# Three engines set to the source's order, with attention dealt out by slots and a third weight group in the sums' place

## The chip, the cores and the metric

One core of a Trainium2 chip runs one launch of the kernel. Its engines work in parallel, each on its own queue of instructions, and wait for one another by semaphores: TensorE (PE) multiplies matrices, VectorE (DVE) and ScalarE (ACT) do elementwise work, GpSimd (POOL) does little here, SyncE (SP) issues nearly all DMAs. The metric is device time in microseconds (us), the median of several executions.

## The reference

A transformer block in which attention and a feed-forward part stand side by side, in float32, for 2048 tokens of 576 features:

```python
x = A_x                                   # [1, 2048, 576]
xn = _layernorm(x, axis=-1)
return x + _A_ref(xn, A_wqkv, A_wo) + _B_ref(xn, B_w1, B_b1, B_w2, B_b2)

def _A_ref(x, wqkv, wo):                  # 32 heads of 18, 8 keys each, every second token back
    W, dil = 8, 2
    ...
    idx = pos[:, None] - off[None, :]
    ...
    logits = jnp.einsum("bhsd,bhswd->bhsw", q, kg) * scale
    logits = jnp.where(mask[None, None, :, :], logits, -1e9)
    attn = _softmax(logits, axis=-1)
    o = jnp.einsum("bhsw,bhswd->bhsd", attn, vg)
    return (lambda x, *d: x.transpose(*d))(o, 0, 2, 1, 3).reshape(B, S, D) @ wo

def _B_ref(x, w1, b1, w2, b2):            # 576 -> 4608 -> 576
    h = jnp.einsum("bsd,df->bsf", x, w1) + b1
    r = jnp.where(h > zero, h, zero)
    h = r * r
    return jnp.einsum("bsf,fd->bsd", h, w2) + b2
```

## The kernel before

**Numbers.** TensorE multiplies in a rounded 32-bit format. To keep float32's accuracy each operand is split in two: ScalarE writes the rounded upper half (`split`, lines 105 to 110), VectorE subtracts it from the original for the lower half (all through `tt`, line 103), and a product is three matmuls. So every weight and every activation that TensorE reads needs one ScalarE and one VectorE instruction first.

**Blocks and stages.** The tokens are four blocks of 512. In order: an opening (layer-norm of block 0 and its first Q, K, V weights); `q0`, the Q, K, V rows of blocks 0 and 1 in four groups of eight heads, 14 matmuls a row; `phase_a(0)`; `phase_b0`; `phase_a(1)`; `phase_b1`; `tail`.

**`phase_a(s)`** is 18 pairs (`ffn_pair`) over the 36 tiles of 128 hidden features. A pair computes two tiles for blocks 2s and 2s+1 at once by a scheme with seven products in place of eight (B11, T1, T2, T3, B21, B22, T4; 50 matmuls with the leftover 64 features), which needs sums of weights (`combine_w1`, VectorE) and sums of activations (`sums`, `last_sum`). Between the products `work(0)` to `work(3)` put seven matmuls each of the second layer of the pair before it, for block 2s. For block 2s+1 the hidden features `h` go out to DRAM and are read back (`load_h`) in `phase_b0` or `phase_b1`, which run that block's second layer, 36 tiles of 14 matmuls. `phase_b0` also computes Q, K, V of blocks 2 and 3.

**Attention** (`attention`, line 258) is done on VectorE for 16 pieces (block b, head group g). Q, K and V go to DRAM scratch and come back as `q` (two buffers) and `kv` (three) with the keys that precede a block. For each of four token columns VectorE multiplies queries with eight shifted keys (`pr<-q,kv`) and sums over 18 features (line 272); then a softmax with ScalarE's exponential (line 279); then four times weights by values (`pr<-lg,kv`) and a sum over the eight (line 288). The result goes to scratch. `regroup` (line 460) reads it back in 16 small DMAs a half, VectorE transposes it, and 65 matmuls apply `wo`.

**What sets the order.** Only TensorE's instructions (and those of the opening and the tail) run in the order of the source. VectorE, ScalarE and SyncE are ordered when the program is built, by a scheduler that fills each engine by priority and readiness; attention stands under `lazily`, at a priority below all else, so its pieces fall wherever that scheduler's model finds VectorE free. Once built, each engine's order is fixed.

**Weights.** `w1` tiles are loaded one pair ahead, split in two instructions (`split_w1`); `w2` tiles are loaded three ahead into `w2r` and split into `w2s` two ahead.

Of the kernel before, what the change touches and what calls it, by code (L numbers as in the profile page):

```python
# [8 lines left out]
F32 = mybir.dt.float32  # L9
# [7 lines left out]
P = 128  # L17
# [24 lines left out]
LATE = 1 << 20  # L42
# [4 lines left out]
def block_kernel(ctx: ExitStack, tc: tile.TileContext, x, xt, wqkv, wo, w1, b1, w2, b2, out):  # L47
# [6 lines left out]

    xv = x.rearrange("(b p j) d -> b p j d", p=P, j=NJ)
# [3 lines left out]
    first = sb.tile([P, 2, TB], F32, name="mb")  # L59
    ident, odd = first[:, 0, :P], first[:, 1].bitcast(F32R)  # L60
# [23 lines left out]

    late = [LATE]

    @contextmanager
    def lazily():
        kept = tc.cur_priority
        tc.cur_priority = late[0]  # L90
        yield
        late[0] = tc.cur_priority
        tc.cur_priority = kept
# [28 lines left out]
    def take_left(to, v, t):  # L122
        nc.scalar.activation(to[:64], v[:64], AF.Copy)
        nc.scalar.activation(t[64:], v[64:], AF.Copy)
        tt(to[64:], v[64:], t[64:].bitcast(F32), ALU.subtract)

# [18 lines left out]

    def statistics(b):
        rows = sb.tile([P, NJ, D], F32, name="kv", bufs=3)
        nc.sync.dma_start(rows, xv[b])
        mr = sb.tile([P, 2, NJ], F32, name="mr")
        for j in range(NJ):  # L150
            for k in range(2):
                bn_stats(b, rows, j, k)
# [3 lines left out]
        nc.sync.dma_start(mrscr[b].rearrange("n p -> p n"), mr.rearrange("p k j -> p (k j)"))  # L156

    def load_xt(b):
        xm[b] = sb.tile([P, NC - 1, TB], F32, name="w1r", bufs=2)
        nc.sync.dma_start(xm[b], xt[b, :, :NC - 1])  # L160
        xf[b] = four()[:, 0] if b % 2 else sb.tile([P, TB], F32, name="xf")
        nc.sync.dma_start(xf[b], xt[b, :, NC - 1])
        mb[b] = sb.tile([P, 2, TB], F32, name="mb")
        nc.sync.dma_start(mb[b].rearrange("c k t -> c (k t)"), flat(mrscr[b], 0, [0, P], 2 * NJ * P))

    def normalize(b):
        open_x(b)
        for a in (0, 2):
# [3 lines left out]
            split(X[b][:, 0, a:a + 2], X[b][:, 1, a:a + 2], v)  # L172
        for k, op in enumerate((ALU.subtract, ALU.mult)):
            tt(xf[b], xf[b], mb[b][:, k], op)
        take_left(x4[b], xf[b], four(F32R)[:, 0])

    def sums(s):
# [3 lines left out]
        v = xm[b1]  # L181
        for i in (1, 2, 3):
            SS[i] = mt.tile([P, 2, 2, TB], F32R, name=f"S{i}")
        f = four()
        tt(f, v[:, :2], v[:, 2:], ALU.add)
        split(SS[1][:, 0], SS[1][:, 1], f)
        e = four()
        tt(e, f, hi(0), ALU.subtract)
        tt(e, e, lo(0), ALU.subtract)
        split(SS[2][:, 0], SS[2][:, 1], e)  # L190
        f = four()
        tt(f, hi(0), v[:, :2], ALU.subtract)
        tt(f, f, lo(0), ALU.add)
        split(SS[3][:, 0], SS[3][:, 1], f)
        tt(v[:, :2], hi(2), e, ALU.subtract)
        tt(v[:, :2], v[:, :2], lo(2), ALU.add)
        x4["d"] = mt.tile([P, TB], F32R, name="x4d")
        tt(xf[b1], xf[b0], xf[b1], ALU.subtract)
        take_left(x4["d"], xf[b1], four(F32R)[:, 0])

    def last_sum(s):
        b = 2 * s + 1
        split(X[b][:, 0, :2], X[b][:, 1, :2], xm[b][:, :2])
# [3 lines left out]
    def load_wq(g):  # L207
        raws[g] = []
        for k in range(3):
            n = 2 if k < 2 else 1  # L210
            r = sb.tile([P, 2, QW], F32, name="r4", bufs=4)[:, :n]
            nc.sync.dma_start(r, wqkv[g, :, 2 * k:2 * k + n])
            raws[g].append(r)

    def split_wq(g, name, ks=range(3)):
        for k in ks:
            n = 2 if k < 2 else 1
            t = mt.tile([P, 2, 2, TB], F32R, name=name, bufs=3)[:, :n, :, :QW]
            wq.setdefault(g, []).append(t)
            split(t[:, :, 0], t[:, :, 1], raws[g][k])  # L220
# [3 lines left out]
    def row_products(b, g, j):  # L224
        js = slice(j * P, (j + 1) * P)
        mm = []
        for c in range(NC):
            w = wq[g][c // 2][:, c % 2]
# [29 lines left out]

    def attention(b, g):
        k, v = (sb.tile([P, NE, CG], F32, name="kv", bufs=3) for _ in range(2))  # L260
        q = sb.tile([P, NJ, CG], F32, name="q", bufs=2)
        nc.sync.dma_start(q.rearrange("p j c -> p (j c)"), flat(scr["q"][g], (PAD + b * TB) * CG, [NJ * CG, P], NJ * CG))
        for t, n in ((k, "k"), (v, "v")):
            nc.sync.dma_start(t.rearrange("p e c -> p (e c)"),
                              flat(scr[n][g], (PAD + b * TB - HALO) * CG, [NJ * CG, P], NE * CG))
# [3 lines left out]
        for j in range(NJ):  # L269
            pr = sb.tile([P, W, CG], F32, name="pr")  # L270
            tt(pr, q[:, j:j + 1].to_broadcast([P, W, CG]), shifted(k, j, [1, CG]), ALU.mult)
            nc.vector.tensor_reduce(out=lg[:, j * HG:(j + 1) * HG].rearrange("p a w -> p w a"),  # L272
                                    in_=pr.rearrange("p w (a d) -> p w a d", d=DH), axis=AX.X, op=ALU.add)
        if b == 0:
# [4 lines left out]
        nc.scalar.activation(lg, lg, AF.Exp, scale=SCALE)  # L279
        nc.vector.tensor_reduce(out=sm, in_=lg, axis=AX.X, op=ALU.add)  # L280
        nc.vector.reciprocal(sm, sm)
        tt(lg, lg, sm[:, :, None].to_broadcast([P, NA, W]), ALU.mult)
        for j in range(NJ):
# [4 lines left out]
            nc.vector.tensor_reduce(out=q[:, j], in_=pr.rearrange("p w c -> p c w"), axis=AX.X, op=ALU.add)  # L288
        nc.sync.dma_start(oscr[b, g].rearrange("(p j) c -> p j c", j=NJ), q)

    raw1, raw2, w1s, w2s, w1v = {}, {}, {}, {}, {}
# [4 lines left out]

    def load_w2(n):
        raw2[n] = sb.tile([P, DE], F32, name="w2r", bufs=3)
        nc.sync.dma_start(raw2[n], w2[n % NF])
# [7 lines left out]
    def split_w1(n, k):  # L307
# [639 lines left out]
```

## Time and profile before

| | us |
|---|---|
| median of 3 runs (1231.02 to 1232.57) | 1232.14 |
| the profiled execution, time | 1232.41 |
| the profiled execution, span of its core | 1230.7 |
| mean granted clock of TensorE | 0.974 |
| TensorE busy | 1142.7 |
| VectorE busy | 933.2 |
| ScalarE busy | 575.1 |

The profile is of one execution. "Busy" leaves out the waiting. In the rows of instructions the start comes first, then the length, the engine and line, and output and inputs with `x` and a count; "[8.92 <-ACT p L387]" says that the engine was idle for 8.92 us before it and that ScalarE's instruction of line 387 on tile `p` ended that. In rows of groups stand busy time and the mean in ns behind the bar. The chain of waits goes back from the last instruction, always to what released it. A window's row has start and end, its length, and busy time with count of TensorE, its weight loads, VectorE, ScalarE and GpSimd, then the granted clock (1 is full speed), the DMA share and GB/s.

### The profile page before, as it was taken

Reading aid. Unit: us, or ns where it says so; the run is one execution under the profiler, and the core shown is the slowest. Engines: PE = TensorE matmul, PEld = TensorE weight load, DVE = VectorE, ACT = ScalarE, POOL = GpSimd, SP = SyncE. Lnnn points to the kernel's source line nnn. Section 1 sums busy time; section 2 is a strip of 40 time slices with the busy share of each in tenths; the row PEclk is TensorE's granted clock in tenths of the full one; section 3 lists DMA queues with packets and bytes.
Section 4 is the critical chain, followed back from the end, with each engine's and each line's share of the span. In section 5 each row is a group of like instructions: output and inputs, shape, how many; then the busy total and the mean of one; then the engine's idle time right before and its main releaser. Section 6 shows DMA issues by size and latency. Waiting matters only on the chain.

```text
span 1230.7 us, 13553 instructions
## 1 busy us (share of the span) xinstructions
PE 1142.7 (93%) x5013; PEld 945.1 (77%) x5013; DVE 933.2 (76%) x1074; ACT 575.1 (47%) x809; POOL 18.3 (1%) x32
## 2 busy tenths in 40 slices
PE   8499697999999999999999968999999999999998
PEld 7499575778777778788888856777777888877887
DVE  7498897999999996499688689999999444463223
ACT  5233455555656656352223234655656656632221
POOL 4000010000000000000000000000000000000000
PEclk9899898999999999999999988999999999999999
DMA  8949474646466346979786846554443344489882
GB/s 312 250 157 209 129 223 138 221 175 213 151 203 222 119 169 196 351 277 349 258 264 230 299 136 231 189 213 157 179 153 119 133 148 144 144 244 331 272 267 91
DMA packets 106369, 254.22 MB, mean 207 GB/s; under 512 B 29248, under 2 KB 56640, under 8 KB 91712
## 3 DMA queue, kind: packets, MB, share of 16 engines
q1 hardware_dynamic: 106016, 253.00, 61.7%
q8 instruction: 39, 0.64, 0.2%
q10 hardware_dynamic: 288, 0.37, 0.1%
q14 instruction: 26, 0.21, 0.1%
HBM read 191.90 MB, written 61.43 MB: 206 GB/s over the span
## 4 chain that ended last, share of the span: by engine, by line
PE 35%; DVE 33%; DMA 13%; issue 9%; ACT 7%; SPq 2%; POOL 0%; DVEq 0%; ACTq 0%; POOLq 0%
PE p L331 21%; PE p L368 9%; DVE q L288 7%; DVE pr L103 7%; DMA w1r<-in_w 5%; PE p L250 4%; DVE h L103 3%; DMA q<-qscr 3%; DVE w1s L103 3%; DVE w2s L103 3%; DVE lg L272 3%; DVE r L103 2%; DVE w1r L103 2%; ACT w2s L113 2%; ACT h L379 2%
## 5 line engine op out<-in xcount | busy, mean ns | idle before, releaser
L331 PE MATMUL p<-h,w2s 128*128 128x512 f32 x2010 | 488.4, 392 | 14.3 <-ACT h L379 4.4
L331 PEld LDWEIGHTS p<-h,w2s 128*128 128x128 f32 x2010 | 378.5, 189 | 99.7 <-ACT h L379 9.1
L368 PE MATMUL p<-X,w1s 128*128 128x512 f32 x864 | 224.9, 397 | 15.2 <-DVE r L103 15.1
L103 DVE TENSOR_TENSOR w2s<-w2r,w2s 128x576 fp32r<-128x576 f32 x164 | 123.4, 755 | 137.7 <-ACT w2s L113 136.5
L113 ACT ACTIVATE w2s<-w2r 128x640 fp32r<-128x640 f32 x164 | 120.3, 736 | 200.4 <-PE p L331 133.5
L368 PEld LDWEIGHTS p<-X,w1s 128*128 128x128 f32 x864 | 163.8, 191 | 54.9 <-DVE r L103 20.9
L368 PE MATMUL p<-S,w1s 128*128 128x512 f32 x648 | 171.9, 402 | 22.8 <-ACT p L387 19.1
L368 PEld LDWEIGHTS p<-S,w1s 128*128 128x128 f32 x648 | 121.7, 191 | 58.6 <-ACT p L387 29.5
L250 PE MATMUL p<-w1s,X 128*128 128x432 f32 x576 | 123.1, 363 | 19.6 <-ACT X L107 15.2
L288 DVE TENSOR_REDUCE q<-pr 128x144 f32<-128x1152 f32 x64 | 139.5, 2179 | 0.5
L250 PEld LDWEIGHTS p<-w1s,X 128*128 128x128 f32 x576 | 109.9, 191 | 26.1 <-ACT X L107 15.6
L375 ACT ACTIVATE r<-r,b1t 128x512 f32<-128x512 f32 x72 | 51.9, 721 | 107.3 <-DVE r L103 107.3
L103 DVE TENSOR_TENSOR pr<-q,kv 128x1152 f32<-128x1152 f32 x64 | 86.6, 1354 | 16.8 <-DMA q<-qscr 16.4
L103 DVE TENSOR_TENSOR h<-r,h 128x1024 fp32r<-128x1024 f32 (+2 forms) x78 | 92.0, 1198 | 9.6 <-ACT r L380 6.5
L103 DVE TENSOR_TENSOR w1s<-w1r,w1s 128x1024 fp32r<-128x1024 f32 x72 | 87.9, 1221 | 10.6 <-ACT w1s L107 10.6
L103 DVE TENSOR_TENSOR r<-p,r 128x512 f32<-128x512 f32 x72 | 49.6, 688 | 50.9 <-ACT r L396 26.7
L103 DVE TENSOR_TENSOR pr<-lg,kv 128x1152 f32<-128x1152 f32 x64 | 87.0, 1359 | 1.0
L272 DVE TENSOR_REDUCE lg<-pr 128x64 f32<-128x1152 f32 x64 | 86.4, 1350 | 0.7
L107 ACT ACTIVATE w1s<-w1r 128x1024 fp32r<-128x1024 f32 x72 | 76.0, 1055 | 15.5 <-DVE w1r L103 12.3
L103 DVE TENSOR_TENSOR w1r<-w1r 128x256 f32<-128x256 f32 (+1 forms) x108 | 55.1, 510 | 33.2 <-DMA w1r<-in_w 32.1
L238 ACT ACTIVATE st<-p 128x432 f32<-128x432 f32 x64 | 32.8, 529 | 101.1 <-PE p L250 58.9
L379 ACT ACTIVATE h<-r 128x1024 fp32r<-128x1024 f32 x72 | 74.2, 1050 | 0.5
(110 smaller groups left out, 869.6 us busy)
## 6 DMA issues: line engine op xcount, KB each, us to landing
h<-h SPq DMA_DIRECT2D x72, 1024.0 KB, 5.3
w2r<-in_w SPq DMA_DIRECT2D x144, 320.0 KB, 3.3
w1r<-in_w SPq DMA_DIRECT2D x36, 640.0 KB, 4.0
kv<-kscr SPq DMA_DIRECT2D x16, 1296.0 KB, 6.9
kv<-vscr SPq DMA_DIRECT2D x16, 1296.0 KB, 7.6
w1r<-in_xt SPq DMA_DIRECT2D x7, 1024.0 KB, 5.3
r<-in_wqkv SPq DMA_DIRECT2D x16, 432.0 KB, 5.5
w2r<-in_wo SPq DMA_DIRECT2D x20, 320.0 KB, 4.8
```

The source lines that it names most:

```text
L103: return nc.vector.tensor_tensor(out=out, in0=a, in1=b, op=op)
L107: i = nc.scalar.activation(hi, raw, AF.Copy)
L113: nc.scalar.activation(w[:, :DE], raw, AF.Copy)
L238: return nc.scalar.activation(stage[g][:, j], p[:, :QW], AF.Copy)
L250: nc.tensor.matmul(p[:, :QW], l, r, start=k == 0, stop=k == len(mm) - 1)
L272: nc.vector.tensor_reduce(out=lg[:, j * HG:(j + 1) * HG].rearrange("p a w -> p w a"), in_=pr.rearrange("p w (a d) -> p w a d", d=DH), axis ...
L288: nc.vector.tensor_reduce(out=q[:, j], in_=pr.rearrange("p w c -> p c w"), axis=AX.X, op=ALU.add)
L331: nc.tensor.matmul(yp[b][c], v, a, start=c not in yb[b], stop=c in last and c not in [o[0] for o in ops[i + 1:]], skip_group_check=True)
L368: nc.tensor.matmul(to, l, r, start=start and i == 0, stop=i == len(mm) - 1, skip_group_check=True)
L375: nc.scalar.activation(to, a, AF.Relu, bias=b1t[:, f:f + 1])
L379: nc.scalar.activation(h[:, 0], r, AF.Square)
```

## The change

1. VectorE, ScalarE and SyncE also run in the source's order, all through the kernel. The scheduler no longer moves their instructions; a DMA is issued where the code says so.
2. `attention`, `statistics`, `normalize`, `sums` and `split_wq` become generators that yield after one piece of work. `side(k)` takes k pieces from a queue of attentions; `run(gens, k)` takes from a list of preparations first, then from that queue. A pair has five slots (one behind T1, two behind B22, two at its end), a tile of `phase_b0` one or two. `offer` puts an attention in the queue, `fetch` issues loads when a `kv` buffer is free, `release` frees one. `complete(b)` runs the queue before `regroup`.
3. `w2` and `wo` become one `stream` with their own counters (`w2_hi`, `w2_lo`), two tiles ahead of TensorE, its load three ahead. Loads of `h` and `w1` are placed by hand two or three ahead.
4. A pair's last square and its lower halves of `h` move into the next pair (`finish_pair`); the first pair of a phase ends with T4 ahead of B22.
5. The Q, K, V rows of `q0` run in the order (0,1), (0,3), (0,2), (1,3), (1,2), (1,1), (1,0); the last two rows become filler of the first pair. The split weights of group 3 (in `phase_b0` of groups 0 and 2) lie in the tiles S1 to S3 that later hold the activation sums.
6. The sum over eight keys at line 288 becomes three additions of halves, 576, 288 and 144 elements. The leftover's upper half is written by one ScalarE instruction where there were two.
7. `phase_b0` ends at tile 31 with all preparations, `complete(1)`, both regroups of block 1 and then the offers of block 3's attentions; block 1's projection moves to its end and into the first pair of `phase_a(1)`.

The core of the diff:

```diff
+    ctx.enter_context(tc.manual_schedule(engines={ET.PE, ET.Activation, ET.DVE, ET.SP}))
...
+    def fetch():
+        while free[0] and loads:
+            free[0] -= 1
+            kind, b, g = loads.pop(0)
...
+            t = landed[kind, b, g] = sb.tile([P, NE, CG], F32, name="kv", bufs=3)
+            if kind == "k":
+                q = landed["q", b, g] = sb.tile([P, NJ, CG], F32, name="q", bufs=2)
+                nc.sync.dma_start(q.rearrange("p j c -> p (j c)"),
+                                  flat(scr["q"][g], (PAD + b * TB) * CG, [NJ * CG, P], NJ * CG))
+            nc.sync.dma_start(t.rearrange("p e c -> p (e c)"),
+                              flat(scr[kind][g], (PAD + b * TB - HALO) * CG, [NJ * CG, P], NE * CG))
+
+    def release():
+        free[0] += 1
+        fetch()
+
+    def offer(b, g=None):
...
+            loads.extend([("k", b, g), ("v", b, g)])
+            queue.append((("k", b, g), lambda: attention(b, g)))
+        fetch()
...
     def attention(b, g):
...
             tt(pr, q[:, j:j + 1].to_broadcast([P, W, CG]), shifted(k, j, [1, CG]), ALU.mult)
+            if j == NJ - 1:
+                release()
+            yield
...
-            nc.vector.tensor_reduce(out=q[:, j], in_=pr.rearrange("p w c -> p c w"), axis=AX.X, op=ALU.add)
...
+            yield
+            tt(pr[:, :4], pr[:, :4], pr[:, 4:], ALU.add)
+            tt(pr[:, :2], pr[:, :2], pr[:, 2:4], ALU.add)
+            tt(q[:, j], pr[:, 0], pr[:, 1], ALU.add)
...
+    def side(k, exp=True):
+
+        while k > 0:
+            if current[0] is None:
+                if not queue or queue[0][0] not in landed:
+                    return k
+                current[:] = [queue.pop(0)[1](), None]
+            if current[1] == "exp" and not exp:
+                return k
+            try:
+                current[1] = next(current[0])
+                k -= 1
+            except StopIteration:
+                current[0] = None
+        return 0
+
+    def complete(b):
+        while any(n[0] == "k" and n[1] <= b for n, _ in queue):
+            assert side(1) == 0
+        while current[0] is not None:
+            side(1)
...
+        def finish_pair():
+            r0, r1, h0 = prev.pop("r")
+            h1 = square_hi(r1)
+            square_lo(r0, h0)
+            square(r1)
+            yield
+            square_lo(r1, h1)
...
         product(bc, T1, ss(1), start=True)
+        if before:
+            next(before)
+        if not last:
+            combine_w1(n + 1)
+        if not first:
+            side(1, False)
+        work(0)
...
+            if p == NP - 1:
+                complete(b)
                 regroup(b, 0)
...
+            ffn_pair(s, p, work)
...
     def phase_b0():
...
+            if n == 31:
+                run_all(pieces)
+                last_sum(1)
+                complete(1)
+                load_w1(NP)
+                load_w1(NP + 1)
+                regroup(b, 0)
                 regroup(b, 1)
...
+                for g in range(G):
+                    offer(3, g)
...
+        todo = [(b, g, j) for b, g in ((0, 1), (0, 3), (0, 2), (1, 3), (1, 2), (1, 1), (1, 0)) for j in range(NJ)]
+        pieces = [statistics(1), once(load_mb, 1), split_wq(3, "S", lambda: load_wq(2)), normalize(1)]
```

How it moves instructions, at the places that matter most. First VectorE before, in the last pairs of `phase_a(0)`: the lower halves of `h` (`h<-r4,h`), the drains (`r4<-p7,r4`), the weights (`w1s`, `w2s`) and, between them, one attention's multiplies and sums (`pr`, `q`).

```order
L103 TENSOR_TENSOR pr_1400<-lg_1379,kv_1374 128x1152
L103 TENSOR_TENSOR w1s_3435<-w1r_3376,w1s_3435 128x1024
L288 TENSOR_REDUCE q_1375<-pr_1400 128x144
L103 TENSOR_TENSOR w2s_3373<-w2r_3257,w2s_3373 128x576
L103 TENSOR_TENSOR h_3342<-r4_3306,h_3342 128x1024
L103 TENSOR_TENSOR w2s_3493<-w2r_3378,w2s_3493 128x576
L103 TENSOR_TENSOR pr_1403<-lg_1379,kv_1374 128x1152
L103 TENSOR_TENSOR h_3362<-r4_3307,h_3362 128x1024
```

Here no two rows of attention stand side by side without the pair's own work close by. Now VectorE after the change, from the end of pair 16 of `phase_a(0)` on: the last sums of attention (1,3), written to `q_2402`, and the first rows of (1,2).

```order
L93 TENSOR_TENSOR pr_3383<-lg_2887,kv_2724 128x1152
L93 TENSOR_TENSOR pr_3383<-pr_3383 128x576
L93 TENSOR_TENSOR pr_3383<-pr_3383 128x288
L93 TENSOR_TENSOR q_2402<-pr_3383 128x144
L93 TENSOR_TENSOR pr_3403<-q_2854,kv_2853 128x1152
L347 TENSOR_REDUCE lg_3400<-pr_3403 128x8x8
```

From there on follow only rows of attentions, (1,2), (1,1) and (1,0) whole, 29 each. They end so:

```order
L93 TENSOR_TENSOR pr_3528<-lg_3492,kv_3462 128x1152
L93 TENSOR_TENSOR pr_3528<-pr_3528 128x576
L93 TENSOR_TENSOR pr_3528<-pr_3528 128x288
L93 TENSOR_TENSOR q_3445<-pr_3528 128x144
L93 TENSOR_TENSOR h_3368<-r4_3330,h_3368 128x1024
L93 TENSOR_TENSOR h_3575<-r4_3331,h_3575 128x1024
L93 TENSOR_TENSOR w2s_3592<-w2r_3193,w2s_3592 128x576
```

The two `h` rows are the lower halves that pair 16 leaves; they come behind the three attentions. The second place is the end of `phase_b0`: SyncE after the change at tile 31, where `o_111` and `o_112` are the results of attentions (2,2) and (2,3), `w1r` the first weights of `phase_a(1)`, `o_105` to `o_108` the attention results of block 1 that `regroup` reads, and `qscr_97`, `kscr_89`, `vscr_93` scratch of (3,0).

```order
L372 DMA o_112<-q 128x576
L419 DMA w1r<-in_w 128x1280 x2
L673 DMA st<-o_105 32x4x96 x4
L673 DMA st<-o_106 32x4x96 x4
L673 DMA st<-o_107 32x4x96 x4
L673 DMA st<-o_108 32x4x96 x4
L673 DMA r_5380<-o_105 32x4x48 x4
L673 DMA r_5380<-o_106 32x4x48 x4
L673 DMA r_5380<-o_107 32x4x48 x4
L673 DMA r_5380<-o_108 32x4x48 x4
L318 DMA q<-qscr_97 128x576
L320 DMA kv<-kscr_89 128x2592
```

Before, the same 32 transfers had weight loads between them. VectorE at that place, after the change, right behind the last rows of attention (2,3), where the `w2s` rows are the weights of the tiles 34 and 35:

```order
L93 TENSOR_TENSOR w2s_5407<-w2r_5213,w2s_5407 128x576
L93 TENSOR_TENSOR pr_5429<-q_5398,kv_5397 128x1152
L93 TENSOR_TENSOR w2s_5431<-w2r_5259,w2s_5431 128x576
L347 TENSOR_REDUCE lg_5426<-pr_5429 128x8x8
L93 TENSOR_TENSOR w1r_5359<-w1r_5359 128x512
```

The second row is the first multiply of (3,0), which needs the `q` and `kv` at the end of SyncE's rows above; the subtraction for tile 35 comes behind it.

More of the change, by code (lines that the diff above doesn't have):

```diff
@@ L612, in tail @@
+            side(2)
+        for c in range(NC):
+            w2_hi()
+            add(b, o_ops(b, c), (NC - 2,) if c == NC - 1 else ())
+            w2_lo()
+        tail()
     def tail():
@@ L617, in tail @@
         for n in (NF - 2, NF - 1):
[L618 to L619 removed]
+            ops += tile_products(b, n, h)
         drain(b, e)
```

696 lines of the change are left out of this document (406 added, 290 removed).

## The prediction

> **What bounds the kernel now.** I read the page first: the busy shares, the 40 slices and the groups.
>
> ```profile
> span 1230.7 us, 13553 instructions
> PE 1142.7 (93%) x5013; PEld 945.1 (77%) x5013; DVE 933.2 (76%) x1074; ACT 575.1 (47%) x809; POOL 18.3 (1%) x32
> DVE  7498897999999996499688689999999444463223
> ```
>
> TensorE is busy 93% of the span, so 88 us (1230.7 - 1142.7) is all that any new order can find in its idle time, with a few more where the clock is low. VectorE's 76% is an average: slices 9 to 16 (pairs of blocks 0 and 1) and 25 to 31 are full, the last nine are not. So the question is what each stage waits for. Next the timeline of TensorE and the chain of waits at the ends of the stages, and the busy time by stage.
>
> ```profile
> 131.62 2.92 PE L368 MATMUL p<-S,w1s 128*128 128x512 f32 x6 [8.92 <-ACT p L387]
> 142.19 1.07 PE L368 MATMUL p<-X,w1s 128*128 128x512 f32 x4
> 477.09 8.12 PE L331 MATMUL p<-h,w2s 128*128 128x512 f32 x35
> 718.16 16.98 PE L331 MATMUL p<-w1s,w2s 128*128 128x512 f32 x65 [11.01 <-ACT w1s L107]
> 748.55 2.93 PE L368 MATMUL p<-X,w1s 128*128 128x512 f32 x6 [4.95 <-DVE r L103]
> 754.38 1.52 PE L368 MATMUL p<-X,w1s 128*128 128x512 f32 x6
> 1070.75 4.50 PE L331 MATMUL p<-h,w2s 128*128 128x512 f32 x19
> 950.81 1.66 PE p L368 x6
> 952.92 1.59 PE p L331 x7
> 1005.01 1.66 PE p L368 x6
> 142.00:477.00 335.00, 312.44 (x1321) 249.22 (x1320) 307.21 (x334) 192.39 (x259) 3.12 (x4) 0.98 0.53 177
> 707.00:754.00 47.00, 30.80 (x116) 24.38 (x116) 40.72 (x49) 15.17 (x21) 0.00 (x0) 0.82 0.57 178
> 950.00:1071.00 121.00, 120.37 (x525) 97.78 (x524) 56.10 (x65) 72.77 (x99) 0.00 (x0) 1.00 0.41 141
> ```
>
> In the two rows of windows from 142 and 950 us (TensorE, weight loads, VectorE, ScalarE), the first has VectorE 92% busy, the other 46%. From 142.19 to 477.09 run 17 pairs, 19.70 us each. Once no attention is left, three pairs take 1005.01 - 950.81 = 54.20, or 18.07 each. A pair has 78 matmuls; seven take 1.59 us, 0.227 each, so 17.7 is the least. Before, then, pairs with attention beside them pay 1.6 us each for VectorE's order, and the seams (131, 718, 748 us) pay stalls and a low clock.
>
> **The change, part by part.** The sum is made against the profiled execution, 1232.41 us, which is 0.3 above the median of the three runs (1232.14) and 1.7 above its span. The prices on VectorE come from its groups by form.
>
> ```profile
> L288 DVE TENSOR_REDUCE q<-pr 128x144 f32<-128x1152 f32 x64 | 139.5, 2179 | 0.5
> L103 DVE TENSOR_TENSOR w2s<-w2r,w2s 128x576 fp32r<-128x576 f32 x164 | 123.4, 755 | 137.7 <-ACT w2s L113 136.5
> L103 DVE TENSOR_TENSOR w1s<-w1r,w1s 128x1024 fp32r<-128x1024 f32 x72 | 87.9, 1221 | 10.6 <-ACT w1s L107 10.6
> L103 DVE TENSOR_TENSOR pr<-lg,kv 128x1152 f32<-128x1152 f32 x64 | 87.0, 1359 | 1.0
> L103 DVE TENSOR_TENSOR h<-r,h 128x1024 fp32r<-128x1024 f32 x72 | 86.7, 1223 | 6.5 <-ACT r L380 6.5
> L103 DVE TENSOR_TENSOR pr<-q,kv 128x1152 f32<-128x1152 f32 x64 | 86.6, 1354 | 16.8 <-DMA q<-qscr 16.4
> L272 DVE TENSOR_REDUCE lg<-pr 128x64 f32<-128x1152 f32 x64 | 86.4, 1350 | 0.7
> L103 DVE TENSOR_TENSOR r<-p,r 128x512 f32<-128x512 f32 x72 | 49.6, 688 | 50.9 <-ACT r L396 26.7 <-PE p L368 23.9
> L103 DVE TENSOR_TENSOR w1r<-w1r 128x256 f32<-128x256 f32 x72 | 30.3, 420 | 0.3
> 668.09 1.36 DVE L103 TENSOR_TENSOR pr<-lg,kv 128x1152 f32<-128x1152 f32 x1
> 669.48 2.19 DVE L288 TENSOR_REDUCE q<-pr 128x144 f32<-128x1152 f32 x1
> L279 ACT ACTIVATE lg<-lg 128x256 f32<-128x256 f32 x16 | 6.6, 411 | 18.8 <-DVE lg L103 18.8
> ```
>
> *One attention.* The sum over eight (L288) becomes three adds of 576, 288 and 144 elements. 576 costs 0.755; from 256 (0.420) and 512 (0.688) a subtraction costs 0.15 + 1.05 ns an element, so 288 and 144 come to 0.45 and 0.30, together 1.51 for 2.18. One attention is four multiplies and reductions (4 x (1.354 + 1.350) = 10.8), the softmax (five operations of at most 256 elements like the 0.420 row, 2.1), four multiplies with their adds (4 x 2.87 = 11.5): 24.3 us on VectorE, in 18 pieces of 1.35.
>
> *Pairs.* VectorE's own work in a pair is 2 x 0.755 + 2 x 1.221 + 2 x 1.223 + 2 x 0.688 + 0.688 + 2 x 0.420 = 9.3. Five pieces beside it add 6.8: 16.1, under TensorE's 17.7. Each piece stands where TensorE has other products queued, so I take the free pair's 18.07 for all: 17 x (19.70 - 18.07) = **-28** for blocks 0 and 1 and, from 754.38 to the pairs' end at 1070.75 (18.61 each), **-9** for blocks 2 and 3. Lower bound 17.7 a pair (another -13 in all); upper bound no gain, if a piece lands ahead of a needed subtraction.
>
> ```profile
> 60.09 0.73 PE L250 MATMUL p<-w1s,X 128*128 128x432 f32 x1 [15.21 <-ACT X L107]
> 24.99 5.46 POOL mr L144 x4
> 532.25 5.49 PE p L250 x28
> ```
>
> *Opening.* The 15.21 us stall hangs on block 1's normalisation, a chain (mean scattered, spread again by DMA, normalised) that the change leaves as long, so it stays. The 8.92 stall of the first pair gets the last two Q, K, V rows as filler (28 matmuls, 5.49 us), and the low clock behind it goes, 2.92 for 1.52. I take **-8**, between -12 (2 us more from group 3's own tiles) and +2 (SyncE's loads now queue behind one another).
>
> *The piece at the last pair of blocks 0 and 1.* This decides. Pair 17 begins with `complete(0)`. Its second loop calls `side` until no attention is under way, but `side` opens the next one that is loaded before it returns. So behind the last adds of (1,3), (1,2), (1,1) and (1,0) stand whole, in one piece, on VectorE, ahead of the subtractions of the second halves of `h` for pair 16. 3 x 24.3 + 1.5 = 74.4; 88 gaps of 0.03 (668.09 + 1.36 to 669.48) and three exponentials of 0.41 between VectorE's rows make 78. VectorE comes there about when TensorE ends pair 16. TensorE can then do 29 matmuls of pair 17 (B11, T1, seven of the second layer, T2, two leftovers, two more), 6.6 us, and waits for the second half of `h`: 78 + 1.2 - 6.6 = 73, and 1.4 for the low clock. VectorE's rest for pair 17 then runs 1 late: **+75**. Without the gaps 71; with the longest exposure (no cover) 81. What hides the same work elsewhere is the slots: five pieces a pair, none here. On SyncE the loads of these attentions, sixteen regroup transfers and block 2's loads queue up behind; nobody waits longer for them than for `h`.
>
> ```profile
> 1093.00:1231.00 138.00, 130.83 (x578) 107.27 (x576) 46.53 (x67) 31.98 (x45) 0.00 (x0) 1.00 0.71 234
> 707.30 7.59 SPq L460 DMA_DIRECT2D st<-o  x12
> 714.30 2.16 DMA st<-o
> kv<-kscr SPq DMA_DIRECT2D x16, 1296.0 KB, 6.9
> 636.78 3.74 DMA qscr<-st
> 640.54 9.58 DMA q<-qscr
> 855.25 2.79 PE L368 MATMUL p<-S,w1s 128*128 128x512 f32 x6 [2.21 <-ACT p L387]
> ```
>
> *End of blocks 0 and 1, and of 2 and 3.* The second sixteen regroup transfers are issued behind the first reload of `h`: 16 x 0.63 (twelve in 7.59) = 10.1, landing 2.2, transposes and splits 3. Cover: 63 matmuls of second layer and projection, 14.3, but the subtractions for the last weight chunks stand behind these transposes. I take **+6** each; 0 if the cover holds, +12 if the issue starts only when `h` comes free.
>
> *Second layer of block 1.* VectorE now waits at `pr<-q,kv` for its own block's `q` and `k` just written, 3.74 + 9.58 = 13.3 us, with the next weights' subtractions behind it. Cover: two tiles (28 x 0.227 = 6.4) and the rows between (5.49 for two), 11.9. Three times 1.5 and a low clock at one: **+6**, from 0 to +15.
>
> *Seam at the end of it (n = 31).* The last 17 us of (2,3) and the last sums of block 3 (two of 1.22) stand in one piece, 20, ahead of the weights for tile 34; TensorE has 32 and 33 in hand, so it waits 12. Then SyncE issues 32 regroup transfers (20) ahead of `q` and `k` of (3,0) (1.2 more, landing 6.9, with two weight loads ahead about 31 from the end of the piece), and VectorE's next row is that attention's multiply, ahead of tile 35's subtraction: TensorE, done with tile 34 after 5, waits about 28. Projection chunks and first pair wait 3 each, and the clock costs 5: 51. Before, the stretch 707 to 754 took 47 us for 118 matmuls of 0.227 (26.8): 20 lost. **+31**; at least 0 (the loads overlap), at most +45.
>
> *Last block*: no attention is left, the first regroup stands two tiles later; VectorE busy 46.5 of 138 there before (the window from 1093): **+2** (0 to +5).
>
> Sum: -8 - 28 + 75 + 6 + 6 + 31 - 9 + 6 + 2 = **+81**, 1232.4 + 81 = 1313.4, about 1313.
>
> On the clock the trace and a rule differ. Matmuls after only 2.21 us of waiting took 2.79 for six instead of 1.66. The Trainium skill, "TensorE: Matmul & The Clock Gate", "What's actually happening", has the clock halve after an idle window of about 3.4 us and recover after as long a busy one. By it the two short waits in block 1's second layer cost no clock and the sum is 2 us less, an estimate; by the row they do, and I go by the row.
>
> **The rivals.**
>
> *A. Spread.* The pieces do not run in one block: the queue's order gives way, later VectorE instructions pass the attentions. Place: pair 17 and n = 31. Then +75 and +31 vanish: 1313 - 106 = 1207, faster. It decides from the point where less than 25 of the 106 reach TensorE (the other terms sum to -25). For: VectorE has room later, 46% at 950 us. Against: before, its rows ran in one order with gaps of 0.03, and every stall at VectorE is a wait. 4%.
>
> The Trainium skill, "Perfetto Trace Analysis", "Tensor Engine Instruction (MATMUL, LD_WEIGHTS)", calls the execution queue of VectorE strictly first in, first out, which no row here can show; by it A cannot be.
>
> *B. A cheap seam.* The `k` load of (3,0) is no wait because regroup transfers issue beside it or the piece is short: 28 goes, 1285. For: SyncE had other loads between its regroup rows before. Against: the new order puts all 32 ahead. 17%.
>
> *C. Pairs don't gain.* In-order VectorE makes a ready subtraction wait behind a piece of up to 2.9 us, and pairs stay at 19.7 and 18.6: 1313 + 37 = 1350. For: the first window shows VectorE at 92%. Against: 16.1 of 17.7 fits. 14%.
>
> *D. Only the piece of 75 is smaller*: half of it hidden by something I missed, 1275. 5%.
>
> **How the numbers follow.** My forecast has 60%, from 1295 to 1332 by its own bounds. The range takes in most of B and the near part of C: 1281 to 1344, leaving about 2 in 10 out. About 0.2% (2.5 us) is what a measurement can tell from no change. Faster: A, 0.04. Same: 0.01, where losses and gains happen to cancel. Slower 0.95.
>
> **What would show it.** One TensorE stall of 70 to 80 us around 470, released by VectorE's `h` or ScalarE's, with VectorE full of `pr` rows; pairs from 1.6 us shorter (18.1 each); near 720 to 790 two stalls of some 12 and 28, the second while VectorE waits for `q` or `kv`, with 32 regroup issues ahead of it on SyncE; 15 us still lost at 60; no stall of 9 in the first pair. I am wrong if the long stall is absent or under 50, or if the pairs take over 19.

## The result

The kernel with the change takes 1335.3 us (median of 4 runs, 1334.6 to 1340.04); before, 1231.99 in the same comparison. The ratio is 1.0848, 95% interval 1.0821 to 1.0874: slower by 8.5%. Forecast was 1313, with a range from 1281 to 1344; the forecast's own bounds were 1295 to 1332, and the time lies 3 above them.

The profiled execution is the longest of the four, 1340.04 with a span of 1338.3, 4.7 above the median; all that follows is read from it. The page's busy times and slices after the change:

```profile
span 1338.3 us, 13583 instructions
PE 1149.0 (86%) x5013; PEld 956.9 (72%) x5013; DVE 920.0 (69%) x1202; ACT 572.8 (43%) x800; POOL 13.5 (1%) x32
PE   9397999999999015799989952999999999999978
DVE  6396797887878994474585773788887877442224
```

TensorE's work is the same (1149 against 1143; the mean granted clock is 0.926 for 0.974), but it is busy 86% in place of 93%: 189 us idle against 88. The slices show two holes, in slices 14 to 16 (TensorE 0, 1, 5, VectorE 9, 9, 4) and in 24 and 25. The timeline of TensorE names them:

```profile
64.85 5.06 PE L296 MATMUL p<-h,X 128*128 128x432 f32 x12 [21.16 <-ACT h L251]
125.19 3.33 PE L514 MATMUL p<-X,w1s 128*128 128x512 f32 x6 [7.78 <-ACT w1s L429]
145.21 1.53 PE L514 MATMUL p<-X,w1s 128*128 128x512 f32 x6
429.84 1.52 PE L514 MATMUL p<-X,w1s 128*128 128x512 f32 x6
497.04 2.93 PE L514 MATMUL p<-S,w1s 128*128 128x512 f32 x6 [62.73 <-ACT p L548]
511.07 2.50 PE L483 MATMUL p<-h,w2s 128*128 128x512 f32 x5 [9.67 <-DVE h L93]
522.38 8.37 PE L483 MATMUL p<-h,w2s 128*128 128x512 f32 x35
539.17 6.31 PE L483 MATMUL p<-w1s,w2s 128*128 128x512 f32 x14 [8.43 <-ACT w2s L456]
549.93 14.48 PE L483 MATMUL p<-w1s,w2s 128*128 128x512 f32 x51 [4.44 <-ACT w2s L456]
564.24 13.15 PE L483 MATMUL p<-h,w2s 128*128 128x512 f32 x56
626.43 3.96 PE L483 MATMUL p<-h,w2s 128*128 128x512 f32 x10 [2.09 <-DVE w2s L93]
675.83 4.63 PE L483 MATMUL p<-h,w2s 128*128 128x512 f32 x10 [6.31 <-DVE w2s L93]
720.68 4.63 PE L483 MATMUL p<-h,w2s 128*128 128x512 f32 x10 [3.30 <-DVE w2s L93]
796.64 5.64 PE L483 MATMUL p<-h,w2s 128*128 128x512 f32 x14 [12.23 <-DVE w2s L93]
826.88 4.63 PE L483 MATMUL p<-h,w2s 128*128 128x512 f32 x10 [24.60 <-DVE w2s L93]
862.87 1.53 PE L514 MATMUL p<-X,w1s 128*128 128x512 f32 x6
1163.55 8.37 PE L483 MATMUL p<-h,w2s 128*128 128x512 f32 x35
1287.13 12.49 PE L483 MATMUL p<-h,w2s 128*128 128x512 f32 x42 [7.13 <-DMA h<-h]
```

Pair 17 starts at 429.84 and ends at 522.38. Two waits in it, 62.73 and 9.67, are 72.4 us. ScalarE's and VectorE's timelines show what stood ahead of them:

```profile
470.21 0.42 ACT L355 ACTIVATE lg<-lg 128x256 f32<-128x256 f32 x1 [25.46 <-DVE lg L93]
496.09 0.42 ACT L355 ACTIVATE lg<-lg 128x256 f32<-128x256 f32 x1 [25.46 <-DVE lg L93]
496.41 0.58 ACT L548 ACTIVATE p<-p 128x512 f32<-128x512 f32 x1
```
```profile
432.29 1.36 DVE L93 TENSOR_TENSOR pr<-q,kv 128x1152 f32<-128x1152 f32 x1
...
509.57 0.31 DVE L93 TENSOR_TENSOR q<-pr 128x144 f32<-128x144 f32 x1
509.80 2.35 DVE L93 TENSOR_TENSOR h<-r,h 128x1024 fp32r<-128x1024 f32 x2
```

VectorE works on the three attentions from 432.29 to 509.88, 77.6 us, with nothing else between, and only then on the two lower halves of `h` of pair 16. ScalarE's three exponentials stand ahead of its copy of line 548, so this engine too is held until the third softmax (each exponential starts 25.9 us after the one before). So TensorE's T2 waits for that copy first, and the second layer then waits for `h`.

The second hole is the seam at tile 31. SyncE's and VectorE's timelines there:

```profile
797.42 10.66 SPq L673 DMA_DIRECT2D st<-o  x16
808.12 10.22 SPq L673 DMA_DIRECT2D r<-o  x16
818.38 0.59 SPq L318 DMA_DIRECT2D q<-qscr  x1
819.01 0.43 SPq L320 DMA_DIRECT2D kv<-kscr  x1
```
```profile
795.83 0.75 DVE L93 TENSOR_TENSOR w2s<-w2r,w2s 128x576 fp32r<-128x576 f32 x1
824.79 1.36 DVE L93 TENSOR_TENSOR pr<-q,kv 128x1152 f32<-128x1152 f32 x1 [28.21 <-DMA kv<-kscr]
826.07 0.75 DVE L93 TENSOR_TENSOR w2s<-w2r,w2s 128x576 fp32r<-128x576 f32 x1
```

The 32 regroup transfers take 20.9 us to issue; the load of (3,0) follows, VectorE stands 28.21 us at its multiply, and tile 35's subtraction (826.07) behind it releases TensorE at 826.88.

By stage, from the starts of TensorE's rows before and after (the last row ends with the span):

| stage | before | after | difference | forecast |
|---|---|---|---|---|
| to the second pair | 142.19 | 145.21 | +3.0 | -8 |
| 17 pairs of blocks 0 and 1 | 334.90 | 377.17 | +42.3 | +47 |
| of this: the pairs' pace, 17.79 for 19.70 | | | -32.5 | -28 |
| of this: pair 17 above that pace | | | +74.8 | +75 |
| to block 1's second layer | 22.69 | 41.86 | +19.2 | +6 |
| this layer and the seam, to the second pair | 254.60 | 298.63 | +44.0 | +37 |
| 17 pairs of blocks 2 and 3 | 316.37 | 300.68 | -15.7 | -9 |
| their end and the last block | 159.95 | 174.75 | +14.8 | +8 |
| sum | 1230.7 | 1338.3 | +107.6 | +81 |

(429.84 - 145.21 is 16 pairs, 17.79 each; pair 17 took 92.54; 300.68 / 17 is 17.69.)

### The profile page after: what moved, and what is told of

It reads as the page before. It is cut to its first block, busy times and chain, and to the rows that moved or that the text cites. A ratio compares the mean times of both kernels' runs of the same rounds, so it can differ in the third digit from the quotient of the medians.

```text
span 1338.3 us, 13583 instructions
## 1 busy us (share of the span) xinstructions
PE 1149.0 (86%) x5013; PEld 956.9 (72%) x5013; DVE 920.0 (69%) x1202; ACT 572.8 (43%) x800; POOL 13.5 (1%) x32
## 4 chain that ended last, share of the span: by engine, by line
PE 64%; DVE 15%; DMA 11%; SPq 5%; ACT 2%; issue 2%; DVEq 0%; ACTq 0%
PE p L483 30%; PE p L514 24%; DVE pr L93 7%; PE p L296 4%; PE p L518 4%; SPq L673 3%; DMA qscr<-st 3%; DVE lg L347 2%; DMA h<-h 2%; DMA kv<-kscr 2%; DMA w2r<-in_w 1%; DMA mr<-mr 1%; DVE w2s L93 1%; PE p L973 1%; SPq L289 1%
## 5 line engine op out<-in xcount | busy, mean ns | idle before, releaser
L483 PE MATMUL p<-h,w2s 128*128 128x512 f32 x2010 | 505.1, 401 | 72.1 <-DVE w2s L93 48.5
L483 PEld LDWEIGHTS p<-h,w2s 128*128 128x128 f32 x2010 | 387.6, 194 | 160.8 <-DVE w2s L93 50.7
L514 PE MATMUL p<-X,w1s 128*128 128x512 f32 x864 | 221.4, 392 | 9.4 <-ACT w1s L429 7.8
L514 PE MATMUL p<-S,w1s 128*128 128x512 f32 x648 | 166.9, 393 | 64.5 <-ACT p L548 62.7
L93 DVE TENSOR_TENSOR w1s<-w1r,w1s 128x1024 fp32r<-128x1024 f32 x72 | 88.2, 1225 | 35.4 <-ACT w1s L429 34.4
L347 DVE TENSOR_REDUCE lg<-pr 128x64 f32<-128x1152 f32 x64 | 86.5, 1352 | 1.5
L93 DVE TENSOR_TENSOR pr<-pr 128x576 f32<-128x576 f32 (+1 forms) x128 | 77.6, 607 | 3.4
L483 PE MATMUL p<-w1s,w2s 128*128 128x512 f32 x260 | 66.9, 417 | 15.3 <-ACT w2s L456 15.2
L529 ACT ACTIVATE r<-r 128x1024 f32<-128x1024 f32 x72 | 76.0, 1055 | 1.2
L483 PEld LDWEIGHTS p<-w1s,w2s 128*128 128x128 f32 x260 | 52.2, 203 | 29.6 <-ACT w2s L456 17.8
L93 DVE TENSOR_TENSOR r<-p,r 128x512 f32<-128x512 f32 (+1 forms) x76 | 52.3, 688 | 27.6 <-ACT r L576 14.8
```

Source lines behind the costliest of these rows:

```text
L93: return nc.vector.tensor_tensor(out=out, in0=a, in1=b, op=op)
L483: nc.tensor.matmul(yp[b][c], v, a, start=c not in yb[b], stop=c in last and c not in [o[0] for o in ops[i + 1:]], skip_group_check=True)
L514: nc.tensor.matmul(to, l, r, start=start and i == 0, stop=i == len(mm) - 1, skip_group_check=True)
L529: nc.scalar.activation(r, r, AF.Square)
```

## The experiments

Runs 1 to 4 change one thing in the kernel with the change, 5 to 7 one thing in run 1, 9 and 10 one thing in run 8, which puts 1 and 5 to 7 together. The cuts of the code show the lines that matter; "..." stands for what is left out.

**1. `complete` stops at its own block.** The generator's name is kept in `now`, and the loop ends as soon as neither it nor the queue holds an attention of block b or earlier.

```diff
...
     def complete(b):
-        while any(n[0] == "k" and n[1] <= b for n, _ in queue):
-            assert side(1) == 0
-        while current[0] is not None:
-            side(1)
+        own = lambda n: n is not None and n[0] == "k" and n[1] <= b
+        while own(now[0]) or any(own(n) for n, _ in queue):
+            assert side(1) == 0 or not own(now[0])
```

> complete(b) stops as soon as no attention of block b or earlier is left; later ones stay in the queue for the slots. Theory (the pieces that complete puts in one block are the loss): the stall of pair 17 goes (-75), the seam's 12 and the wait for (3,0)'s load of 25 go, since the queue always holds an attention that has long been loaded, and the waits for q and k in block 1's second layer go (-12): about 1335 - 124 = 1211, 1200 to 1225. Rival (VectorE has no room for the three attentions elsewhere): TensorE waits in block 1's second layer and in the last block instead, 1260 to 1300.

Measured: 1232.23 us (10 runs), ratio to before 0.999, interval 0.997 to 1.0011. The change loses 103 us with this one loop and none without it. TensorE's timeline at the end of the pairs, and what is left at the seam and in the last block:

```profile
446.44 8.41 PE L483 MATMUL p<-h,w2s 128*128 128x512 f32 x35
703.13 5.11 PE L483 MATMUL p<-w1s,w2s 128*128 128x512 f32 x14 [9.63 <-ACT w2s L456]
713.16 8.25 PE L483 MATMUL p<-w1s,w2s 128*128 128x512 f32 x28 [4.92 <-ACT w2s L456]
1061.45 13.53 PE L483 MATMUL p<-w1s,w2s 128*128 128x512 f32 x51 [7.79 <-ACT w2s L456]
1180.43 11.73 PE L483 MATMUL p<-h,w2s 128*128 128x512 f32 x42 [11.30 <-DMA h<-h]
```

The pairs now end at 446.44, 75.9 earlier, the 62.73 and the 24.60 are gone, and no wait for `w2s` by VectorE is left in block 1's second layer. So the theory of the cause stands, and its rival (no room on VectorE) falls as to the size. Its range of 1200 to 1225 was missed by 7, its 1211 by 21: the projection at the seam now waits for the regroup (9.63 + 4.92), and block 3's attentions, now later, run into the last block (their last result goes out at 1159.51; with the change at 1117.67, still beside the pairs), where reloads of `h` come behind regroup (11.30). In block 1's second layer a wait of 3.21 us for ScalarE's `st` is new.

**2. The first door only.** `complete` as in run 1, with one more loop that leaves tile 31 as it was.

```diff
+        while b and current[0] is not None:
+            side(1)
```

> As the run before for phase_a(0), but at tile 31 of block 1's second layer complete still empties the queue. Theory: the piece only moves; 94 rows of attention stand at tile 31 in place of about 23, some 78 us of VectorE in place of 20, so the seam loses 58 more while pair 17 wins 75 and the waits for q and k win up to 12: about 1306, 1295 to 1325, with one TensorE stall of 65 to 75 near tile 34. Rival (pair 17 is held by SyncE's regroup and loads, not by the piece): the stall at pair 17 stays over 40 and the time is 1350 or more.

Measured: 1308.03 us (2 runs), ratio to before 1.0605, 1.0544 to 1.0666, where 1306 was expected. TensorE's timeline at tile 33 and on:

```profile
756.14 2.07 PE L485 MATMUL p<-h,w2s 128*128 128x512 f32 x4 [68.58 <-ACT w2s L458]
769.56 5.19 PE L485 MATMUL p<-h,w2s 128*128 128x512 f32 x14 [11.35 <-DVE w2s L93]
800.44 4.21 PE L485 MATMUL p<-h,w2s 128*128 128x512 f32 x10 [25.68 <-DVE w2s L93]
```

The piece only moved: no stall at pair 17, one of 68.58 at the seam, with the two known ones behind it. Again ScalarE's split behind the third exponential ends the long wait and VectorE's subtraction behind the piece the next (11.35). In both places the piece costs about its length, and SyncE's regroup, which is still issued at pair 17, had no part in the 72 us.

**3. One sum in place of three additions.**

```diff
-            tt(pr[:, :4], pr[:, :4], pr[:, 4:], ALU.add)
-            tt(pr[:, :2], pr[:, :2], pr[:, 2:4], ALU.add)
-            tt(q[:, j], pr[:, 0], pr[:, 1], ALU.add)
+            nc.vector.tensor_reduce(out=q[:, j], in_=pr.rearrange("p w c -> p c w"), axis=AX.X, op=ALU.add)
```

> The three additions go back to one sum over eight (2.18 for 1.51 us). Theory (pairs are TensorE-bound with VectorE at 16 to 17 of 17.8): only the pieces on TensorE's path grow, 16 sums x 0.67 = 11, so about 1346, 1341 to 1352, pairs still under 17.95. Rival (VectorE sets the pace everywhere): 64 x 0.67 = 43, 1378.

Measured: 1353.31 us (2 runs), ratio 1.0972, 1.091 to 1.1035: 18 more than with the additions by the medians (15 by the ratios), just above the theory's 1341 to 1352 and far from the rival's 1378. The additions are no cause of the loss, but win 15 to 18. The pairs keep 17.79 us (16 of them from 148.34 to 432.98), so VectorE does not set their pace. TensorE's two waits in pair 17 are 68.34 + 11.44, 7.4 more, for twelve longer sums in the piece. More stands where VectorE's attention is ahead of a weight in block 1's second layer and the seam (8.71, 4.87 and 14.19 for 6.31, 3.30 and 12.23); the expectation had counted the last of these alone. The first pair's wait is 10.2 for 7.8, but it is 7.8 to 9.2 in other runs with the same rows there, so not all of this is the edit.

**4. The loads of (3,0) ahead of the regroup.**

```diff
+                for g in range(G):
+                    offer(3, g)
                 regroup(b, 0)
                 regroup(b, 1)
-                for g in range(G):
-                    offer(3, g)
```

> At tile 31 the offers of block 3's attentions stand ahead of the 32 regroup transfers. Theory (the second stall of the seam is SyncE's issue time ahead of (3,0)'s load): the 24.6 us wait falls to under 8, and what needs the regroup is 2 later: about 1317, 1312 to 1322. Rival (the projection waits for the regroup anyway and takes the wait over): 1330 to 1336.

Measured: 1334.7 us (2 runs), ratio 1.0821, 1.0758 to 1.0885: no gain, as the rival had it (1330 to 1336). TensorE's waits at the seam behind the one of 12.23, which stays, and two rows of the chain of waits:

```profile
808.66 4.63 PE L483 MATMUL p<-h,w2s 128*128 128x512 f32 x10 [6.54 <-DVE w2s L93]
825.34 4.92 PE L483 MATMUL p<-w1s,w2s 128*128 128x512 f32 x14 [12.04 <-ACT w2s L456]
835.39 8.19 PE L483 MATMUL p<-w1s,w2s 128*128 128x512 f32 x28 [5.14 <-ACT w2s L456]
```
```profile
799.39 15.87 DMA kv<-kscr
815.27 0.54 SPq L673
```

The 24.60 fell to 6.54, as the theory has it, but the projection then waits 12.04 and 5.14 for the regroup. The edit itself made the regroup later: seven of its transfers go out behind the loads, and the eighth only when the last of these loads, the `kv` issued at 799.39, has landed at 815.26 (run 5 looks at this). The 32 are issued by 831.2, where with the change they were by 818.3. So the run shows that the wait moves to the regroup under this order; how much of the 18 us an undelayed regroup would have won was not tried.

**5. Reload of `h` behind the regroup** (on top of run 1).

```diff
-        load_h(s, 0)
         next(end)
         regroup(b, 1)
+        load_h(s, 0)
```

> The run with complete stopping at its own block (1232), and at the end of phase_a the first reload of h stands behind the sixteen regroup transfers, not ahead. Theory (the ninth small transfer waits until the slow reload of h, one of eight transfers that SyncE may have under way, has landed, 12 to 16 us): the projection's two stalls at the end of blocks 0 and 1 (3.9 + 5.0, and 3 of low clock) and of blocks 2 and 3 (7.8) go, 1232 - 18 = 1214, 1210 to 1220. Rival (sixteen issues of 0.65 and the landing are too long by themselves): under 6 us, 1227 to 1232.

Measured: 1232.04 us (10 runs), ratio 0.9996, 0.9985 to 1.0006: no gain, where 1214 was expected. The chain of waits in run 1, and then in this run:

```profile
448.22 12.17 DMA h<-h
460.41 0.54 SPq L673
```
```profile
446.24 11.72 DMA w2r<-in_wo
457.97 0.54 SPq L673
```

In run 1 seven of the sixteen transfers go out behind the reload of `h`, and the eighth starts when that reload has landed (the expectation, one off, says the ninth); nine then follow at once. In this run the eighth starts when a load of projection weights has landed, the transfer issued just ahead of the sixteen. So a transfer waits for the one eight places ahead, like in a ring of eight, but the edit only changed which slow transfer sits there. The two stalls of 3.93 and 4.99 became one of 9.37, and the 7.79 at the end of blocks 2 and 3 became 5.27. The time is at the rival's upper end (1227 to 1232), but not for its reason: sixteen issues alone do not explain a start that waits for a landing.

**6. Opening loads behind block 1's statistics** (on top of run 1).

```diff
-    load_w1(0)
     free[0] = 2
-    offer(0, 0)
...
-        pieces = [statistics(1), once(load_mb, 1), split_wq(3, "S", lambda: load_wq(2)), normalize(1)]
+        pieces = [statistics(1), once(load_w1, 0), once(offer, 0, 0), once(load_mb, 1), split_wq(3, "S", lambda: load_wq(2)), normalize(1)]
```

> The run with complete stopping at its own block (1232), and the load of w1 and of the first q, k and v are issued behind block 1's statistics (mr), not ahead. Theory (mr's small packets queue behind some 3.5 MB that SyncE now issues ahead of them, 17.7 us to land where before it took 9.7): mr lands 6 to 8 earlier and the stall at 64 us falls from 20.4 to some 14: 1225, 1222 to 1228. Rival (mr is slow by its own 4-byte packets): 1230 to 1234.

Measured: 1229.56 us (6 runs), ratio 0.9966, 0.995 to 0.9981; 3 less than run 1, but the two intervals overlap, and the time lies between the theory's range (to 1228) and the rival's (from 1230). The stall falls from 20.38 to 15.05, as before the change, but 2.76 of it comes back at 37.6 us, where TensorE waits for group 3's split. The theory holds for the stall; its gain in time is not clear of noise.

**7. The first pair's weights ahead of the rows of (1,0)** (on top of run 1).

```diff
                 combine_w1(0)
+                for k in range(2):
+                    w1_hi(0, k)
+                    w1_lo(0, k)
...
-            if r in (24, 25):
-                w1_hi(0, r - 24)
-                w1_lo(0, r - 24)
-            else:
+            if r < 24:
                 run(pieces, 3 if r < 4 or 15 <= r < 20 else 2)
```

> The run with complete stopping at its own block (1232), and the first pair's weights are split ahead of the rows of (1,0), not between them. Theory (ScalarE's split stands behind a copy of a row that waits 8 us until the row tile's former content has gone to DRAM): the 8.8 stall of the first pair goes, 1224, 1221 to 1227. Rival (the weights themselves are late, or TensorE's rows then wait for the same copy): 1230 to 1234.

Measured: 1223.97 us (4 runs), ratio 0.9924, 0.9909 to 0.9938; 8 less than run 1, as expected. The wait of the first pair for `w1s` falls from 8.75 to 2.91; what is left hangs on VectorE's sums of these weights, for which ScalarE's split waits 6.35. The theory holds: in run 1 ScalarE copied a row ahead of the split, and that copy waited 12.16 us for the row tile's transfers to DRAM.

**8. All together**, and in the last block regroup's transfers in fours over tiles 22 to 27, with the loads of `x` for the residual moved to tile 26.

```diff
             if n == 22:
                 complete(b)
-                regroup(b, 0)
+            if n in range(22, 26):
+                regroup(b, 0, [n - 22])
+            if n in range(24, 28):
+                regroup(b, 1, [n - 24])
+            if n == 26:
                 residual(b)
                 residual_left(b)
-            if n == 25:
-                regroup(b, 1)
```

> All four edits (complete at its own block, reload of h behind regroup, opening loads behind mr, weights split first), and in the last block regroup's 32 transfers are spread over the tiles 22 to 27 in fours. If each gains by itself: 1232 - 18 - 7 - 8 - 12 (the stalls of 11.3 and 2.6 in the last block) = 1187, 1180 to 1200, faster than both kernels. Rival (the waits only move on to the next in-order engine): 1205 to 1225.

Measured: 1220.14 us (4 runs), ratio 0.9893, 0.9874 to 0.9911. It is 1.1% faster than before and beats both kernels, but by less than the sum of 1187; the time is in the rival's range (1205 to 1225), by which the waits only move on. So the last block's did (1.41, 8.13 and 1.54 in place of 11.30 and 2.62), and run 5's edit gave nothing.

**9. Block 2's loads behind the second regroup** (on top of run 8).

```diff
                 residual(b)
-                if s == 0:
-                    load_xt(2)
-                    load_mb(2)
...
         load_h(s, 0)
+        if s == 0:
+            load_xt(2)
+            load_mb(2)
```

> The run with all edits (1220), and block 2's loads (1 MB of x and the spread means) move from ahead of pair 17's end to behind the second regroup. Theory (the ninth regroup transfer waits for whatever slow transfer has its place in the ring of eight, and the projection's weight is slow because the large load stands ahead of it): the stall of 10.0 at 457 falls under 4 with its low clock, 1211, 1207 to 1215. Rival (the loads of h, q and k alone fill the DMA engines there): 1217 to 1223.

Measured: 1219.84 us (4 runs), ratio 0.9894, 0.9876 to 0.9912: nothing won in the time, where 1211 was expected. The stall of 9.99 there became 4.01 and 3.27, and the eighth transfer still waits for a projection weight that takes 10.05 (11.51 in run 8). So the large loads are not, in the main, what makes that load slow; what does was not found. The rival's time came (1217 to 1223), but its cause, that the loads of `h`, `q` and `k` fill the DMA engines, was not tested. Of the 2.7 won there, 0.5 is left at the seam (the first wait there ends at 693.57 for 694.05).

**10. Half of the seam's regroup from ScalarE's queue** (on top of run 8): the second `regroup` of tile 31 uses `nc.scalar.dma_start`.

```diff
-                regroup(b, 1)
+                regroup(b, 1, q=nc.scalar)
```

> The run with all edits (1220), and at tile 31 the second half of regroup is issued by ScalarE's queue beside SyncE's. Theory (the seam's two stalls, 9.3 and 4.3, are 32 issues of 0.64 on one queue): together under 5, 1220 - 9 = 1211, 1207 to 1215. Rival (ScalarE's own split of the next weights now stands behind its sixteen issues, 10 us, and TensorE waits for that): 1218 to 1228.

Measured: 1214.33 us (4 runs, 1210.46 to 1219.83), ratio 0.9848, 0.9816 to 0.988. The runs are spread and the interval overlaps that of run 8, so 6 us is not a firm size. The time lies in the theory's range (1207 to 1215), but the theory's sign did not come, two waits together under 5: 9.31 and 4.25 became 10.63 and 1.33, the first now for ScalarE's split of a tile's weights, which stands behind this engine's issues of transfers, as the rival had it. Most of the wait changed engine, and the time fell all the same.

## Why the prediction was right

*What decides.* Right, place and size. The piece at pair 17 was put at 78 us of VectorE and +75; it took 77.6 without the last adds of (1,3), 79.2 with them (from 430.66), and +74.8. Run 2 moves the piece and the loss goes with it, run 3 makes it longer and the loss there grows by 7.4. So rival D (half of it hidden) falls. One detail was wrong: TensorE was to stop at the lower half of `h`, after 29 matmuls, in one wait; it stopped after 19, at T2, for ScalarE's copy behind the exponentials, and met `h` after the 29. The sum, 73 of waits, came out at 72.4, since both end with the piece.

*Pairs.* -28 and -9 were forecast, -32.5 and -15.7 came: pairs run at 17.79 and 17.69, at the lower bound of 17.7, not at the old free pair's 18.07. In that free pair ScalarE's copy for T2 stood behind the squares of the pair before and a weight's split (965.71 to 968.24), and T2 started 0.24 us late, at 968.87; with the change the copy starts ahead of the last two of them (1113.71). That this is the whole gain of 0.3 to 0.4 a pair was not tested. Rival C (pairs stay at 19.7) falls.

*The seam.* 12 and 28 were forecast as waits, 12.23 and 24.60 came. The projection, put at waits of 3, then waited only 0.65, 1.08 and 0.56, since the regroup landed while the load of (3,0) was awaited. With the low clock behind them (fourteen matmuls in 5.64 and ten in 4.63 us, some 2.2 more than at full clock each) the two waits are 41.3; from there to the second pair it took 31.36 (from 831.51), where it took 47.23 before (from 707.15). So the seam lost 25, an estimate, where +31 was forecast. Rival B priced the seam without the load's wait at -28. Run 4 took 18 off that wait and won nothing, but it delayed the regroup as well, so B's price was neither borne out nor settled.

*Too low were* four terms, together by 44; the seam's 6 and the pairs' 11 on the other side leave the 27 that are missing in the profiled execution. So the distance of 22 us to the median is what is left of larger errors of both signs, and that it stayed inside the range is in part luck: the range went up to 1344 for the sake of rival C, which did not come. The opening (-8, came +3): the chain of block 1's statistics was not "as long" as before. The stall behind it grew from 15.21 to 21.16, and `w1` and three attention loads went out ahead of its 4 KB scatter (the last section has the rows). The first pair's old stall of 8.92 went as forecast, but a new in-order wait of 7.78 came in its place. Run 6 shows the first, run 7 the second. The end of blocks 0 and 1 (+6, came +19): the prediction counted issue and landing of sixteen transfers, and not that the eighth waits for a slow load under way (15.81 us for `h`):

```profile
524.63 15.81 DMA h<-h
540.46 0.54 SPq L673
```

Block 1's second layer (+6, came about +19, the 44 less the seam's 25): three waits behind loads of `q` and `k` of 2.09, 6.31 and 3.30 where three of 1.5 were counted, and a low clock after each where one was (ten matmuls in 3.96, 4.63 and 4.63 us). The end of blocks 2 and 3 and the last block (+8, came +15): the end took 1 more than before (23.7 from 1163.55 to 1187.25) where 6 was forecast; the last block had a wait of 7.13 for `h` behind regroup that was not foreseen.

*The clock.* The prediction went by the row for short waits, and the measurement bears it out here: after a wait of 2.09 us ten matmuls took 3.96 us (row 626.43), at a granted clock of 0.60; at full clock ten take 2.4 (nine take 2.20 at 852.00). By the rule of the Trainium skill ("TensorE: Matmul & The Clock Gate", "What's actually happening") the clock halves after an idle window of about 3.4 us; by it this row would have run at full clock, so the measurement decides. The prediction's sum has this clock at one of the three waits, 1.4 us, so the 2 us by which it set the rule apart are 1.4. But the length of a wait does not settle it: after 2.59 us in run 10 twelve matmuls ran at a granted clock of 1.00 (2.61 us), after 1.89 us in run 4 ten ran at 0.64 (3.76 us).

*Rival A* (the queue gives way) falls: VectorE's two `h` rows follow the last `q` row, 0.23 us after its start, though what the first of them needed was ready at 431.11, 78.7 us before. The two stalls came where the order put them.

## What to carry to other kernels

When an engine is put in source order, look for every loop that drains a queue, and ask what it drains beyond what the next step needs: here one loop condition was worth 103 us, and the rest of the change was worth nothing to before until the in-order waits behind it were moved (12 us, run 8). A stall in such an order is priced by the length of the piece ahead on its engine less the work in hand on the waiting one; the same sum has to be made for every engine that has a row in the piece (ScalarE's exponentials here). Before removing a wait, look for the next one that ends close behind it, and for what the edit itself delays: in runs 5 and 9 another slow transfer took the place of the first, in run 4 the loads moved ahead held up the transfers behind them.

## What the runs showed of the hardware that was not expected

On SyncE's queue a transfer did not start before the one eight places ahead of it had landed. At five places that show it (pair 17's end with the change, runs 1, 5 and 9 there, run 4 at the seam) seven transfers went out behind a slow one that took 10.05 to 15.87 us, and the eighth within 0.02 us of its landing. Whether the program or the chip sets the eight is not shown.

A small transfer can take long when large loads are issued ahead of it. SyncE's timeline before, and then after the change, for the scatter of block 1's statistics (`mr<-mr`) and the transfer that waits for it to land (`mb<-mr`):

```profile
30.47 0.38 SPq L156 DMA_DIRECT2D mr<-mr  x1
40.28 0.32 SPq L164 DMA_DIRECT2D mb<-mr  x1
```
```profile
30.18 0.38 SPq L320 DMA_DIRECT2D kv<-vscr  x1
30.65 0.52 SPq L146 DMA_DIRECT2D mr<-mr  x1
48.34 0.33 SPq L161 DMA_DIRECT2D mb<-mr  x1
```

Issued at nearly the same time, the scatter of 4 KB held the next for 9.8 us before and for 17.7 with the loads of `w1`, `q`, `k` and `v` ahead of it. In runs 6 and 8, where these went out behind it, it took 13.2 and 13.8. So their place explains about 4 of the 8 us; the rest is open.

VectorE's sum over eight, whose inputs lie 144 elements apart, took 2179 ns before; its sum over 18 neighbours with as many inputs took 1352 ns (line 347). The three additions of 1008 elements together take 1.60 us from start to end in the attention alone (447.47 to 449.07). The two sums also differ in their number of outputs, 144 and 64, so that the distance is the reason is likely, not shown.
